# Memory attention, then a mixture of experts: z and M loaded once per batch, the first k and beta on the scalar queue, PSUM banks taken in turn by name, and a new step order

## The chip, the core and the metric

The kernel runs on one core of a Trainium2 chip. Five engines with a queue each work beside one another: TensorE (PE, matrix products and transposes), VectorE (DVE), ScalarE (ACT), GpSimd (POOL) and SyncE (SP, which here only issues transfers). An engine takes its instructions in order and waits at the head of its queue until the semaphores that an instruction names are there. The metric is the time of one execution on the device in microseconds (us), from three runs.

## The reference

Softmax attention and a linear memory are mixed by a gate per head; a router normalised eight times spreads the result over eight experts.

```python
B, H, S, D = 4, 8, 576, 64
a = softmax(where(causal, -1e9, scale * q @ k.T))
local = a @ v
phi = lambda x: where(x > 0, x, exp(x) - 1) + 1
mem_out = (phi(q) @ M_prev) / (phi(q) . z_prev + 1e-6)
g = 1 / (1 + exp(-beta))                    # one number for each head
x = g * mem_out + (1 - g) * local           # (2304, 512)
P = exp(x @ w_gate - max); 8 times: rows, then columns of P normalised, P *= N / E
out = sum over e of P[:, e] * (relu(x @ w1[e]) @ w2[e])
```

## The kernel before, in words

**Attention.** The 32 (batch, head) problems are taken as 16 pairs, pair p holding heads 2hp and 2hp+1 of batch b (`b, hp = divmod(p, 4)`), one head in each half of the 128 partitions. A pair is some 70 small steps that `steps(p)` names: `lq`, `lk`, `lv`, `lz`, `lm` load q, k, v, z_prev and M_prev by transfers of SP; `tq`, `tk`, `t5` transpose q and k on PE; `hq`, `hk`, `h5` (ACT) and `l_q`, `l_k`, `l5` (DVE) split them into a high and a low part; `s2`, `s3`, `s1`, `s4` are the scores of the row tiles (three products each); `m` (DVE) masks and takes the maxima; `x` (ACT) is the exponential with its sums; `rd`, `rv`, `rm` (DVE) make the reciprocals `rr` of the sums; `tr` transposes `rr`; `t30`, `t31`, `t20`, `t21`, `t1`, `t0`, `t4` transpose the exponentials, and `c..`, `d..`, `e0`, `e1` copy them from PSUM to `eA`, `eB`, `e1`, `e3`, `e4t`, on ACT or DVE as the table `TAKE` says; `fe`, `fm`, `fa`, `fz`, `ns`, `nr` are phi(q) and its norm against z; `gn`, `gp`, `tn`, `tp`, `cn`, `cp` scale and transpose phi; `v0` and `v1` are the products with v and M_prev in the PSUM bank `x`, `cx`, `km`, `kh`, `kl` take them out into the tensors `xh` and `xl`.

**Order.** Nothing is scheduled by the compiler here. Each step of pair p has the place p + WHEN[name] (+ LATER); all steps of all pairs are sorted by it, and each engine's queue is what remains of that list. A step that belongs to pair p can thus stand after steps of pair p + 1. From place 5.33 on, pieces of the first expert (`first1`, `first2`: products of PE in the bank `f`, 12 or 6 of 512 columns) are set between the steps, two for each pair, and the router's logits; pairs 1 to 4 have no such piece and are called plain below.

**Buffers.** The program uses eight PSUM banks: `x`, `f` and six that `ps_s()` hands out (tag `s`, bufs=6) to the transposes and the scores. A step that is given a bank waits until the readers of what stood there are through. `eA`, `eB`, `e1`, `e3`, `e4t` and `tmp` exist once; q, k and v are loaded into two buffers each. `z` has two buffers and three transfers a pair (a broadcast over 128 partitions and two halves of 64), `M_prev` three buffers and two transfers a pair. The start sends beta (in `setup_gates`) and then pair 0's q, z and k through SP.

**After attention** the expert loop (`experts`) has six products of 512 columns or twelve of 384 back to back on PE, in 71 items.

Of the kernel before, what the change touches and what calls it, by code (L numbers as in the profile page):

```python
# [17 lines left out]
def kernel(  # L18
# [70 lines left out]
    gt = ca.tile([128, 2, H], F32, name="gt")  # L89

    def ps_s():
        return ps.tile([128, 512], F32, tag="s", name="s", bufs=6)

    ps_t = ps_s

    def f32(ap):
# [3 lines left out]
    def w_task(j):  # L100
        dst = slots[0]
        if j < 2:
            hi, lo = (dst[a][:, 2 * j:2 * j + 2].rearrange("p k f -> p (k f)")
                      for a in ("w1h", "w1l"))
        else:
            hi, lo = dst["w2h"][:, j - 2], dst["w2l"][:, j - 2]
        raw = []

        def load():
            raw.append(wst_p.tile([128, 512], F32, tag="wst", name="wst"))  # L110
# [32 lines left out]

    def setup_gates():
        nc.sync.dma_start(
            out=gt[:, 0, :], in_=beta.rearrange("(o h) -> o h", o=1).to_broadcast([128, H])
        )
        nc.scalar.activation(out=gt[:, 0, :], in_=gt[:, 0, :], func=AF.Exp, scale=-1.0)
        nc.vector.tensor_scalar_add(gt[:, 0, :], gt[:, 0, :], 1.0)
# [12 lines left out]
    def setup_router():  # L162
        nc.vector.memset(f32(wgp), 0.0)
        wgr = wst_p.tile([128, 512], F32, tag="wst", name="wst")
# [10 lines left out]
    WHEN = {  # L175
# [15 lines left out]
    }  # L191
    LATER = {
    }
    TAKE = {
        "c30": "A", "c31": "D", "e0": "D", "e1": "A", "c20": "A", "c21": "D", "c1": "A",
        "d1": "D", "c0": "A", "d0": "D", "c4": "A", "d4": "D",
    }


    def attention():  # L200
        with ExitStack() as actx:
# [7 lines left out]
            )  # L209
            zb2 = [ap1.tile([128, 2, 128], F32, name=f"zb{j}") for j in range(2)]  # L210
            mraw = [ap1.tile([128, 128], F32, name=f"mraw{j}") for j in range(3)]
            eA = ap1.tile([128, 2, GA], F32, name="eA")
# [7 lines left out]
            for t_ in (*qraw, *kraw, *vraw):  # L220
                nc.vector.memset(t_[:, 4, :], 0.0)
            for t_ in (*mraw, *zb2, qn4, e4t):
                nc.vector.memset(t_, 0.0)
# [16 lines left out]

            def load_kv(p, src, dst):
                b, hp = divmod(p, HP)
                for h in range(2):
                    nc.sync.dma_start(
                        out=dst[:, 0:4, half[h]],
                        in_=src[b, 2 * hp + h, 0:512, :].rearrange("(t p) d -> p t d", p=128),
                    )
                nc.sync.dma_start(
                    out=dst[0:64, 4, :].rearrange("p (h d) -> p h d", h=2),
                    in_=src[b, 2 * hp:2 * hp + 2, 512:576, :].rearrange("h p d -> p h d"),  # L250
                )

            def load_z(p):
                b, hp = divmod(p, HP)
                nc.sync.dma_start(
                    out=zb2[p % 2][:, 0, :],
                    in_=z_prev[b, 2 * hp:2 * hp + 2, :].rearrange("(o h) d -> o (h d)", o=1)
                    .to_broadcast([128, 128]),
                )
                for h in range(2):  # L260
                    nc.sync.dma_start(
                        out=zb2[p % 2][half[h], 1, half[h]],
                        in_=z_prev[b, 2 * hp + h:2 * hp + h + 1, :].to_broadcast([64, 64]),
                    )

            def load_m(p):
                b, hp = divmod(p, HP)
                for h in range(2):
                    nc.sync.dma_start(out=mraw[p % 3][half[h], half[h]], in_=m_prev[b, 2 * hp + h])

            copy_ = {"A": nc.scalar.copy, "D": nc.vector.tensor_copy}

            def steps(p):
# [14 lines left out]

                step("lq")(lambda: load_q(p))
                step("lk")(lambda: load_kv(p, k, kraw[p % 2]))  # L290
                step("lv")(lambda: load_kv(p, v, vraw[p % 2]))
                step("lz")(lambda: load_z(p))
                step("lm")(lambda: load_m(p))

# [36 lines left out]

                zb = zb2[p % 2]

                @step("fe")
# [17 lines left out]
                def _():  # L352
                    nc.gpsimd.tensor_tensor(
                        out=s["tmp"][:, 0:4], in0=s["phi"][:, 0:4],
                        in1=zb[:, 0:1].to_broadcast([128, 4, 128]), op=ALU.mult,
                    )
                    nc.gpsimd.tensor_tensor(
                        out=s["tmp"][:, 4], in0=s["phi"][:, 4], in1=zb[:, 1], op=ALU.mult
                    )

                @step("ns")
                def _():
# [4 lines left out]
                    )  # L367
                    nc.vector.reduce_sum(rm[:, 8:9], tmp[:, 4], axis=AX.X)

# [15 lines left out]
                def scores(name, tiles):  # L385
# [19 lines left out]
                    for i in tiles:  # L405
# [4 lines left out]
                        def _(i=i, w=w, c0=c0):  # L410
                            sp = s.pop(("s", i))
                            s["e", i] = et = ap1.tile(
                                [128, 2, 512], F32, tag="e", name="e", bufs=4
                            )
# [153 lines left out]

                @step("tr")
                def _():  # L570
                    s["tr"] = t_ = ps_t()
                    nc.tensor.transpose(t_[0:9, 0:128], s["rr"][:, 2], ident)

                @step("tn")
                def _():
                    nc.tensor.transpose(s["tr"][:, 128:256], qn4, ident)

# [41 lines left out]
                for grp in range(2):  # L619
# [5 lines left out]
                    def _(grp=grp, w=w):  # L625
# [14 lines left out]
                        for h in range(2):  # L640
                            nc.tensor.matmul(  # L641
                                out=x[half[h], 0:256], lhsT=mraw[p % 3][:, half[h]],
                                rhs=qp[:, 256 * grp:256 * grp + 256], start=False,
                                stop=(grp == 0),
                            )
                        if grp:
                            for h in range(2):
                                nc.tensor.matmul(
                                    out=x[half[h], 256:320], lhsT=mraw[p % 3][:, half[h]],
                                    rhs=qp[:, 512 + 64 * h:576 + 64 * h], start=False, stop=True,  # L650
# [27 lines left out]
            for c, parts in enumerate(early_parts()):  # L678
# [7 lines left out]
            seq.append((WHEN["sg"], setup_gates))  # L686
            seq.append((1.0, setup_router))
# [143 lines left out]
    def first2(c, j, ps_new):  # L831
# [6 lines left out]
        def take():  # L838
            yst = wst_p.tile([128, DM], F32, tag="wst", name="wst")
            nc.vector.tensor_copy(out=yst, in_=bank[0])  # L840
            bank.append(yst)
# [362 lines left out]
```

## Time and profile before

| | |
|---|---|
| median of three runs | 1743.95 us (1743.18 to 1744.05) |
| the profiled execution's own time | 1743.34 us |
| its span, first to last instruction | 1741.5 us |
| PE busy | 1714.7 us, 98% of the span |
| attention, to 260.4 us | PE idle for 21 us |
| expert loop, from 260.4 us | PE idle for 5.8 us |

An engine's busy time is the union of its instructions' spans. The chain of waits goes back from the last instruction to whatever released it, so a line's share in it is the time that this line held up the end. The idle time before an instruction is put down to the semaphore that came last.

### The profile page before, as it was taken

To read this page: it belongs to the slowest core of one execution; us is meant where nothing else is said; L and a number is where in the kernel's file an instruction comes from. 1 tells how busy PE (TensorE), PEld (TensorE's weight loads), DVE (VectorE), ACT (ScalarE), POOL (GpSimd) and SP (SyncE) were. 2 spreads that over 40 slices of the span, in tenths; PEclk is the share of its full clock that TensorE was granted. 3 is DMA by queue.
4 is the path that set the end of the run, shared out by engine and by line. 5 is a ranking of instruction groups with operands and counts; after the bars stand their busy time and mean duration, and the time that the engine had idled before them with its cause. 6 is when DMAs were issued, how large, how long until landed. Compare 5 with 4: busy or idle time off the path is not lost.

```text
span 1741.5 us, 26964 instructions
## 1 busy us (share of the span) xinstructions
PE 1714.7 (98%) x9381; PEld 1524.1 (88%) x9381; DVE 1266.8 (73%) x2359; ACT 693.7 (40%) x1568; POOL 1154.5 (66%) x1107
## 2 busy tenths in 40 slices
PE   6899999999999999999999999999999999999999
PEld 5687778899999999989999999998899999999998
DVE  7877865877777777777777777777777777777776
ACT  5767752343333333234333333333343333333332
POOL 3855654477667777567767677665766777767673
PEclk9999999999999999999999999999999999999999
DMA  4433425122122221223222221222242222222211
GB/s 110 108 99 95 117 61 167 52 73 61 61 73 73 73 62 62 77 86 120 61 67 73 73 69 60 66 73 73 65 132 71 73 73 65 63 67 73 73 61 49
DMA packets 154888, 135.55 MB, mean 78 GB/s; under 512 B 71424, under 2 KB 121728, under 8 KB 154752
## 3 DMA queue, kind: packets, MB, share of 16 engines
q1 hardware_dynamic: 154320, 133.05, 25.9%
q8 instruction: 74, 1.21, 0.3%
q10 hardware_dynamic: 432, 0.79, 0.1%
q14 instruction: 62, 0.51, 0.1%
HBM read 124.28 MB, written 9.51 MB: 77 GB/s over the span
## 4 chain that ended last, share of the span: by engine, by line
PE 93%; DVE 1%; ACT 1%; DMA 0%; issue 0%; POOL 0%; SPq 0%; ACTq 0%; POOLq 0%; DVEq 0%
PE s L826 44%; PE s L1012 29%; PE f L1012 10%; PE x L636 2%; PE s L397 1%; PE s L478 1%; PE f L805 1%; PE f L826 1%; PE s L444 1%; PE x L641 1%; PE s L703 0%; PE s L805 0%; PE s L300 0%; PE s L529 0%; DMA raw<-in_moe_w_dram 0%
## 5 line engine op out<-in xcount | busy, mean ns | idle before, releaser
L963 POOL TENSOR_TENSOR w1l<-raw,w1h 128x512 fp32r<-128x512 f32 x263 | 366.4, 1407 | 395.3 <-ACT w1h L962 391.2
L1083 DVE SCALAR_TENSOR_TENSOR acc<-s,P,acc 128x512 f32<-128x512 f32 x540 | 395.2, 744 | 145.2 <-PE s L826 145.2
L826 PE MATMUL s<-w2h,hhl 128*128 128x512 f32 x1116 | 436.1, 391 | 0.0
L826 PE MATMUL s<-w2l,hhh 128*128 128x512 f32 x1116 | 435.8, 391 | 0.0
L826 PE MATMUL s<-w2h,hhh 128*128 128x512 f32 x1116 | 435.0, 390 | 0.0
L1043 DVE TENSOR_TENSOR temps<-s,temps 128x384 f32<-128x384 f32 x447 | 242.6, 555 | 172.9 <-ACT w1h L962 85.1
L997 DVE SCALAR_TENSOR_TENSOR hhl<-temps,hhh 128x384 fp32r<-128x384 f32 x340 | 306.5, 901 | 0.0
L986 POOL TENSOR_TENSOR w2l<-raw,w2h 128x512 fp32r<-128x512 f32 x186 | 293.3, 1598 | 9.8 <-ACT w2h L985 9.8
L996 ACT ACTIVATE hhh<-temps 128x384 fp32r<-128x384 f32 x340 | 178.6, 525 | 296.9 <-DVE temps L1043 289.4
L826 PEld LDWEIGHTS s<-w2h,hhl 128*128 128x128 f32 x1116 | 209.4, 188 | 43.9
L826 PEld LDWEIGHTS s<-w2h,hhh 128*128 128x128 f32 x1116 | 209.6, 188 | 42.7 <-DVE acc L1083 1.5
L826 PEld LDWEIGHTS s<-w2l,hhh 128*128 128x128 f32 x1116 | 209.4, 188 | 41.6
L1046 ACT COPY temps<-s 128x384 f32<-128x384 f32 x64 | 30.7, 480 | 415.7 <-PE s L1012 408.9
L1012 PE MATMUL s<-th,w1h 128*128 128x384 f32 x510 | 170.3, 334 | 0.0
L1012 PE MATMUL s<-tl,w1h 128*128 128x384 f32 x510 | 170.3, 334 | 0.0
L1012 PE MATMUL s<-th,w1l 128*128 128x384 f32 x510 | 170.3, 334 | 0.0
L1012 PE MATMUL s<-xh,w1l 128*128 128x384 f32 x480 | 161.3, 336 | 0.4 <-POOL w1l L958 0.4
L1012 PE MATMUL s<-xh,w1h 128*128 128x384 f32 x480 | 161.3, 336 | 0.0
L1012 PE MATMUL s<-xl,w1h 128*128 128x384 f32 x480 | 160.8, 335 | 0.0
L962 ACT CAST w1h<-raw 128x512 fp32r<-128x512 f32 x263 | 154.0, 615 | 2.9 <-issue 2.9
L1043 DVE TENSOR_TENSOR temps<-f,temps 128x384 f32<-128x384 f32 x148 | 80.3, 555 | 57.5 <-PE f L1012 27.9
L985 ACT CAST w2h<-raw 128x512 fp32r<-128x512 f32 x186 | 111.9, 607 | 0.0
(218 smaller groups left out, 2873.1 us busy)
## 6 DMA issues: line engine op xcount, KB each, us to landing
raw<-in_moe_w_dram SPq DMA_DIRECT2D x372, 256.0 KB
rsb<-rd SPq DMA_DIRECT2D x32, 144.0 KB
ydr<-wst SPq DMA_DIRECT2D x18, 256.0 KB
acc<-ydr SPq DMA_DIRECT2D x18, 256.0 KB
qraw<-in_q_dram SPq DMA_DIRECT2D x32, 128.0 KB
kraw<-in_k_dram SPq DMA_DIRECT2D x32, 128.0 KB
vraw<-in_v_dram SPq DMA_DIRECT2D x32, 128.0 KB
out_dram<-acc SPq DMA_DIRECT2D x15, 256.0 KB
```

Of the source, the lines that this page charges most:

```text
L636: nc.tensor.matmul(out=x[half[h], a0:a1], lhsT=vs[:, kt, h], rhs=ee(h), start=(kt == 0), stop=False,)
L826: nc.tensor.matmul(out=pt, lhsT=h_[:, f, cols], rhs=w[:, f], start=(n == 0), stop=(n == 5))
L962: nc.scalar.copy(out=wh[:, i:i + 2], in_=src)
L963: tt(out=wl[:, i:i + 2], in0=src, in1=f32(wh[:, i:i + 2]), op=ALU.subtract)
L985: nc.scalar.copy(out=wh[:, j], in_=raws[j])
L986: nc.gpsimd.tensor_tensor(out=wl[:, j], in0=raws[j], in1=f32(wh[:, j]), op=ALU.subtract)
L996: nc.scalar.activation(out=hh[:, f, c], in_=src, func=AF.Relu)
L997: late.append(lambda: nc.vector.scalar_tensor_tensor(out=hl[:, f, c], in0=src, scalar=0.0, in1=f32(hh[:, f, c]), op0=ALU.max, op1=ALU.subt ...
L1012: nc.tensor.matmul(out=pt[:, 0:HT], lhsT=w[:, wi, k], rhs=x[:, k], start=(n == 0), stop=(n == total - 1),)
L1043: nc.vector.tensor_tensor(out=o, in0=x, in1=y, op=ALU.add)
L1046: nc.scalar.copy(out=X, in_=prod(q, [(0, b11)]))
L1083: nc.vector.scalar_tensor_tensor(out=acc[:, j], in0=pt, scalar=P[:, t_, e:e + 1], in1=acc[:, j], op0=ALU.mult, op1=ALU.add,)
```

## The change

- `load_z` and `load_m` run once per batch (`hp == 0`): one broadcast transfer of 512 numbers to 128 partitions (`zb`), and two transfers that fill `mb` for four pairs, in place of twelve and eight. `fz` is one GpSimd instruction over 640 columns and not two of 512 and 128. `ns` reduces the two half tiles of row tile 4 apart.
- `setup_gates` loses its transfer: `load_gates` (place -2.255) issues beta on ACT's queue. Pair 0's k is issued on ACT's queue too.
- `ps_s()` and the staging tiles take their buffers in turn by name (`s0` to `s5`, `wst0`, `wst1`), and the exponentials' tiles have a name for each row tile.
- The bank of `tr` and `tn` is taken by whichever comes first.
- `WHEN` has new numbers throughout, `LATER` gets 24 shifts for pairs 0, 1 and 15, and `TAKE` moves `c21`, `d1`, `d0` and `d4` from DVE to ACT and swaps `e0` (now ACT) and `e1` (now DVE).

```diff
 def ps_s():
-    return ps.tile([128, 512], F32, tag="s", name="s", bufs=6)
+    turn[0] += 1
+    return ps.tile([128, 512], F32, tag=f"s{turn[0] % 6}", name="s", bufs=1)
...
-def setup_gates():
-    nc.sync.dma_start(
+def load_gates():
+    nc.scalar.dma_start(
...
-    step("lk")(lambda: load_kv(p, k, kraw[p % 2]))
+    step("lk")(lambda: load_kv(p, k, kraw[p % 2], nc.sync if p else nc.scalar))
...
-    step("lz")(lambda: load_z(p))
-    step("lm")(lambda: load_m(p))
+    if hp == 0:
+        step("lz")(lambda: load_z(p // HP))
+        step("lm")(lambda: load_m(p // HP))
...
     nc.gpsimd.tensor_tensor(
-        out=s["tmp"][:, 0:4], in0=s["phi"][:, 0:4],
-        in1=zb[:, 0:1].to_broadcast([128, 4, 128]), op=ALU.mult,
-    )
-    nc.gpsimd.tensor_tensor(
-        out=s["tmp"][:, 4], in0=s["phi"][:, 4], in1=zb[:, 1], op=ALU.mult
+        out=s["tmp"], in0=s["phi"],
+        in1=zb[:, hp:hp + 1].to_broadcast([128, 5, 128]), op=ALU.mult,
     )
...
-    nc.vector.reduce_sum(rm[:, 8:9], tmp[:, 4], axis=AX.X)
+    for h in range(2):
+        nc.vector.reduce_sum(
+            rm[half[h], 8:9], tmp[half[h], 4, half[h]], axis=AX.X
+        )
...
-    "c30": "A", "c31": "D", "e0": "D", "e1": "A", "c20": "A", "c21": "D", "c1": "A",
-    "d1": "D", "c0": "A", "d0": "D", "c4": "A", "d4": "D",
+    "c30": "A", "c31": "D", "e0": "A", "e1": "D", "c20": "A", "c21": "A", "c1": "A",
+    "d1": "A", "c0": "A", "d0": "A", "c4": "A", "d4": "A",
```

What the tables make of the queues, at three places. `L469` before and `L480` after is the helper that does the copies of `TAKE`.

ACT at the start of the program, before: the table load, a first exponential, the gate's exponential (`gt`), then pair 0's `fe`, `hq`, `h5`, `hk`.

```order
L142 ACT_TABLE_LOAD
L142 ACTIVATE mx<-ones 128x1
L148 ACTIVATE gt<-gt 128x8
L337 ACTIVATE tmp<-qraw_119 128x640
L304 CAST qh<-s 128x512
L323 CAST kh<-s 128x64
```

The same place after, with beta's transfer ahead of the table load and k's three between the two exponentials.

```order
L154 DMA gt<-in_beta_dram 128x8
L151 ACT_TABLE_LOAD
L151 ACTIVATE mx<-ones 128x1
L261 DMA kraw_121<-in_k_dram 128x4x64 x2
L265 DMA kraw_121<-in_k_dram 64x2x64
L159 ACTIVATE gt<-gt 128x8
L348 ACTIVATE tmp<-qraw_119 128x640
L317 CAST qh<-s 128x512
L317 CAST kh<-s 128x512
```

k's transfers leave SP and stand on ACT, ahead of the gate's exponential, for which DVE's first steps wait.

DVE in a plain pair before, around the reciprocals: `nr` (the last instruction of it), `rd`, the next pair's `l_q`, `rv`, `rm`, `cr`, and after that parts of `l5`, `d4` and `l_k`.

```order
L375 TENSOR_TENSOR rm<-rm,gcol 128x9
L543 TENSOR_SCALAR rr<-sum 128x9
L287 TENSOR_TENSOR ql<-s,qh 128x512
L550 RECIPROCAL rr<-rr 128x9
L548 TENSOR_TENSOR rr<-rm,rr 128x9
L580 COPY rt<-s 9x128
L287 TENSOR_TENSOR kl<-s,kh 128x64
```

The same place after, from `fa` of the next pair on.

```order
L357 SCALAR_TENSOR_TENSOR phi<-qraw_119,tmp 128x640
L554 TENSOR_SCALAR rr<-sum 128x9
L561 RECIPROCAL rr<-rr 128x9
L559 TENSOR_TENSOR rr<-rm,rr 128x9
L299 TENSOR_TENSOR ql<-s,qh 128x512
L299 TENSOR_TENSOR kl<-s,kh 128x512
```

The next pair's `l_q`, which waits for ACT's `hq`, stood between `rd` and `rv`; now `rd`, `rv` and `rm` stand together ahead of it.

PE in a plain pair before, from `tr` to the next pair's scores: `tr`, `t4`, `t30`, `t1`, `tn`, `t0` (two rows), `tp`, `t31`, then `s2` of the next pair.

```order
L572 MATMUL s<-ident,rr 9x128
L529 MATMUL s<-ident,e_135 128x128 x4
L478 MATMUL s<-ident,e 128x128 x4
L497 MATMUL s<-ident,e 128x128 x4
L576 MATMUL s<-ident,qn_136 128x128
L511 MATMUL s<-ident,e 128x128 x2
L514 MATMUL s<-ident,e_135 64x128
L611 MATMUL s<-ident,phi 128x128 x4
L478 MATMUL s<-ident,e 128x128 x4
L397 MATMUL s<-kh,qh 128x384 x2
```

The same place after: `tr`, then `t30`, `t31` and `t20` in one row, `tn`, `t4`, `t1`, `t0`, `s2`.

```order
L586 MATMUL s<-ident,rr 9x128
L489 MATMUL s<-ident,e 128x128 x11
L588 MATMUL s<-ident,qn_133 128x128
L540 MATMUL s<-ident,e_132 128x128 x4
L508 MATMUL s<-ident,e 128x128 x4
L522 MATMUL s<-ident,e 128x128 x2
L525 MATMUL s<-ident,e_132 64x128
L408 MATMUL s<-kh,qh 128x384 x2
```

`tp` has left this place (it stands behind the next pair's `s1` now), `t20` has come here from before `tr`, and `t31` has moved from the end to the front.

## Rows read from the trace of the kernel before

**Rows 1.** The page: busy times by engine, and the chain that ended last

```profile
PE 1714.7 (98%) x9381; PEld 1524.1 (88%) x9381; DVE 1266.8 (73%) x2359; ACT 693.7 (40%) x1568; POOL 1154.5 (66%) x1107
...
PE 93%; DVE 1%; ACT 1%; DMA 0%; issue 0%; POOL 0%; SPq 0%; ACTq 0%; POOLq 0%; DVEq 0%
```

**Rows 2.** Stretches: length; busy of PE, PEld, DVE, ACT, POOL; clock; DMA; GB/s

```profile
0.00:26.80 26.80, 14.84 (x81) 12.14 (x82) 18.20 (x72) 13.58 (x37) 8.76 (x19) 0.94 0.43 95
26.80:82.95 56.15, 50.15 (x446) 38.53 (x445) 47.05 (x170) 41.38 (x127) 39.59 (x51) 1.00 0.46 114
82.95:260.44 177.49, 174.50 (x1429) 139.24 (x1428) 133.75 (x481) 118.92 (x361) 100.86 (x139) 1.00 0.36 94
260.44:1741.50 1481.06, 1475.26 (x7429) 1334.19 (x7429) 1067.81 (x1638) 519.82 (x1045) 1005.31 (x899) 1.00 0.24 74
...
23.64:27.05 3.41, 3.41 (x18) 2.78 (x18) 2.56 (x8) 2.10 (x6) 2.08 (x2) 0.50 0.30 56
```

**Rows 3.** What PE waited for: total us, times, longest

```profile
PE s L572 <- DVE rr L548: 5.2, 5, 2.2
...
PE s L317 <- DMA kraw<-in_k_dram: 3.5, 1, 3.5
PE s L611 <- DVE e L469: 2.2, 4, 0.6
...
PE s L300 <- DVE mn L454: 1.1, 1, 1.1
...
PE s L723 <- ACT ls L711: 0.7, 1, 0.7
```

**Rows 4.** Timeline, SP at the start: start, us taken, engine, line, names

```profile
0.74 0.39 SPq L145 DMA_DIRECT2D gt<-in_beta_dram  x1
...
5.20 1.14 SPq L244 DMA_DIRECT2D kraw<-in_k_dram  x2
6.38 0.66 SPq L248 DMA_DIRECT2D kraw<-in_k_dram  x1
```

**Rows 5.** Timeline of ACT, DVE and PE at the start, to the second pair's scores

```profile
2.02 0.20 ACT L142 ACTIVATE mx<-ones 128x1 f32<-128x1 f32 x1
...
3.58 0.17 DVE L149 TENSOR_SCALAR gt<-gt 128x8 f32<-128x8 f32 x1 [0.49 <-ACT gt L148]
...
6.98 0.69 DVE L287 TENSOR_TENSOR ql<-s,qh 128x512 fp32r<-128x512 f32 x1
...
8.98 0.45 PE L317 MATMUL s<-ident,kraw 128*128 128x128 f32 x1 [3.53 <-DMA kraw<-in_k_dram]
...
11.89 0.69 PE L397 MATMUL s<-kl,qh 64*128 64x384 f32 x2
...
26.80 0.55 PE L397 MATMUL s<-kh,qh 64*128 64x384 f32 x2
```

**Rows 6.** Timeline of DVE and PE in a plain pair

```profile
50.40 0.69 DVE L287 TENSOR_TENSOR ql<-s,qh 128x512 fp32r<-128x512 f32 x1 [0.18 <-ACT qh L304]
...
51.00 0.20 DVE L550 RECIPROCAL rr<-rr 128x9 f32<-128x9 f32 x1
...
51.26 0.28 PE L572 MATMUL s<-ident,rr 128*9 128x128 f32 x1 [0.79 <-DVE rr L548]
```

**Rows 7.** The copies in 37.18:79.27: xcount, busy us, mean ns, idle before

```profile
L469 ACT COPY eB<-s 128x384 f32<-128x384 f32 x9 | 4.0, 482 | 2.6 <-PE s L478 2.5
...
L469 ACT COPY eA<-s 128x256 f32<-128x256 f32 x6 | 2.2, 373 | 4.1 <-DVE e L469 4.1
...
L469 ACT COPY e<-s 128x128 f32<-128x128 f32 x3 | 0.8, 283 | 0.0
...
L469 DVE COPY eB<-s 128x384 f32<-128x384 f32 x6 | 3.3, 556 | 0.5 <-ACT e L469 0.5
...
L469 DVE COPY e<-s 128x128 f32<-128x128 f32 x6 | 1.7, 287 | 3.7 <-ACT eB L469 3.7
...
L469 DVE COPY e<-s 128x256 f32<-128x256 f32 x3 | 1.2, 415 | 0.0
```

More of the change, by code (lines that the diff above doesn't have):

```diff
@@ L89, with wst @@
     gt = ca.tile([128, 2, H], F32, name="gt")
+    turn = [0]
     def ps_s():
-        return ps.tile([128, 512], F32, tag="s", name="s", bufs=6)
+        turn[0] += 1
+        return ps.tile([128, 512], F32, tag=f"s{turn[0] % 6}", name="s", bufs=1)
     ps_t = ps_s
+    wturn = [0]
+    def wst(w=512):
+        wturn[0] += 1
+        return wst_p.tile([128, w], F32, tag=f"wst{wturn[0] % 2}", name="wst", bufs=1)
     def f32(ap):
@@ L109, in load @@
         def load():
-            raw.append(wst_p.tile([128, 512], F32, tag="wst", name="wst"))
+            raw.append(wst())
             if j < 2:
@@ L142, in setup, with setup_gates @@
         nc.scalar.activation(out=mx[:, 0:1], in_=ones[:, 0:1], func=AF.Exp)
-    def setup_gates():
-        nc.sync.dma_start(
+    def load_gates():
+        nc.scalar.dma_start(
             out=gt[:, 0, :], in_=beta.rearrange("(o h) -> o h", o=1).to_broadcast([128, H])
         )
+    def setup_gates():
         nc.scalar.activation(out=gt[:, 0, :], in_=gt[:, 0, :], func=AF.Exp, scale=-1.0)
@@ L163, in setup_router @@
         nc.vector.memset(f32(wgp), 0.0)
-        wgr = wst_p.tile([128, 512], F32, tag="wst", name="wst")
+        wgr = wst()
         wgv = wgr[:, 0:KD * E].rearrange("p (k e) -> p k e", e=E)
@@ L209, in attention @@
             )
-            zb2 = [ap1.tile([128, 2, 128], F32, name=f"zb{j}") for j in range(2)]
-            mraw = [ap1.tile([128, 128], F32, name=f"mraw{j}") for j in range(3)]
+            zb = ap1.tile([128, HP, 128], F32, name="zb")
+            mb = ap1.tile([128, HP, 128], F32, name="mb")
             eA = ap1.tile([128, 2, GA], F32, name="eA")
@@ L221, in attention @@
                 nc.vector.memset(t_[:, 4, :], 0.0)
-            for t_ in (*mraw, *zb2, qn4, e4t):
+            for t_ in (mb, qn4, e4t):
                 nc.vector.memset(t_, 0.0)
@@ L239, in load_q, with load_kv @@
                     )
-            def load_kv(p, src, dst):
+            def load_kv(p, src, dst, eng=nc.sync):
                 b, hp = divmod(p, HP)
                 for h in range(2):
-                    nc.sync.dma_start(
+                    eng.dma_start(
                         out=dst[:, 0:4, half[h]],
@@ L247, in load_kv @@
                     )
-                nc.sync.dma_start(
+                eng.dma_start(
                     out=dst[0:64, 4, :].rearrange("p (h d) -> p h d", h=2),
@@ L251, in load_kv, with load_z, load_m @@
                 )
-            def load_z(p):
-                b, hp = divmod(p, HP)
+            def load_z(b):
                 nc.sync.dma_start(
-                    out=zb2[p % 2][:, 0, :],
-                    in_=z_prev[b, 2 * hp:2 * hp + 2, :].rearrange("(o h) d -> o (h d)", o=1)
-                    .to_broadcast([128, 128]),
+                    out=zb.rearrange("p x d -> p (x d)"),
+                    in_=z_prev[b].rearrange("(o h) d -> o (h d)", o=1).to_broadcast([128, H * D]),
                 )
+            def load_m(b):
                 for h in range(2):
                     nc.sync.dma_start(
-                        out=zb2[p % 2][half[h], 1, half[h]],
-                        in_=z_prev[b, 2 * hp + h:2 * hp + h + 1, :].to_broadcast([64, 64]),
-                    )
[L266 to L269, printed above, removed]
+                        out=mb[half[h], :, half[h]],
+                        in_=m_prev[b, h:H:2].rearrange("x d e -> d x e"),
+                    )
             copy_ = {"A": nc.scalar.copy, "D": nc.vector.tensor_copy}
@@ L330, in _ @@
                     sub(kl[:, 576:704], t_[:, 128:256], s["kh"][:, 576:704])
-                zb = zb2[p % 2]
                 @step("fe")
@@ L412, in _ @@
                             s["e", i] = et = ap1.tile(
-                                [128, 2, 512], F32, tag="e", name="e", bufs=4
+                                [128, 2, 512], F32, tag=f"et{i}", name="e", bufs=1
                             )
@@ L567, in _, with tr_ @@
                     )
[L569 to L576, printed above, removed]
+                def tr_():
+                    if "tr" not in s:
+                        s["tr"] = ps_t()
+                    return s["tr"]
+                step("tr")(
+                    lambda: nc.tensor.transpose(tr_()[0:9, 0:128], s["rr"][:, 2], ident)
+                )
+                step("tn")(lambda: nc.tensor.transpose(tr_()[:, 128:256], qn4, ident))
                 @step("cr")
@@ L641, in _ @@
                             nc.tensor.matmul(
-                                out=x[half[h], 0:256], lhsT=mraw[p % 3][:, half[h]],
+                                out=x[half[h], 0:256], lhsT=mb[:, hp, half[h]],
                                 rhs=qp[:, 256 * grp:256 * grp + 256], start=False,
@@ L648, in _ @@
                                 nc.tensor.matmul(
-                                    out=x[half[h], 256:320], lhsT=mraw[p % 3][:, half[h]],
+                                    out=x[half[h], 256:320], lhsT=mb[:, hp, half[h]],
                                     rhs=qp[:, 512 + 64 * h:576 + 64 * h], start=False, stop=True,
@@ L685, in attention @@
                     seq += [(t0 + WHEN.get(a, 0.0), f) for a, f in zip(kinds, fs)]
-            seq.append((WHEN["sg"], setup_gates))
+            seq += [(WHEN["sl"], load_gates), (WHEN["sg"], setup_gates)]
             seq.append((1.0, setup_router))
@@ L838, in take @@
         def take():
-            yst = wst_p.tile([128, DM], F32, tag="wst", name="wst")
+            yst = wst(DM)
             nc.vector.tensor_copy(out=yst, in_=bank[0])
```

36 rows, old and new, of tables (LATER, WHEN) are left out of this document.

## The prediction

> **What bounds the kernel now.** I read the page's busy times and its chain first [rows 1]: PE is busy for 98% of the span and holds 93% of the chain, so only time in which PE idles, or runs at the lower clock, can be won; the number of products doesn't change. Then the stretches [rows 2], to see where the 27 us of PE's idle time lie. The expert loop has 5.8 us of it in 1481 (1481.06 - 1475.26) and no line of it is changed. Attention has 21: 12.0 up to the second pair's scores (26.80 - 14.84), 6.0 in the four plain pairs (56.15 - 50.15), and 3.0 in the pairs that carry expert pieces (177.49 - 174.50). What may change is therefore in the first 260 us. Then what PE waited for there [rows 3]: the reciprocals of the sums before `tr` (L572, five times), the first k (3.5 us), the copies before `tp` (L611), and a bank in pair 0. Last the timeline at the two places where these waits lie [rows 4 to 6].
>
> **First k (term 1).** SP issues pair 0's k at 5.20, behind eight other transfers (beta, four of q, three of z), and its last part, issued at 6.38, lets PE go on at 8.98, 2.60 later [rows 4, 5]. After, ACT issues it. ACT is through with the table load and its first exponential at 2.22 (2.02 + 0.20); beta's issue ahead costs 0.39 [rows 4], so k is issued from 2.61, two in 1.14 and one in 0.66, the last from 3.75: it lands at about 6.35, some 2.6 earlier. But ACT comes to the gate's exponential only after the third issue, at 4.41, and DVE's first steps wait for that: they begin at about 4.65 (4.41, the exponential's 0.20 and a little) instead of 3.58. From 3.58 to the end of `l_q` at 7.67 (6.98 + 0.69) they took 4.09, so `l_q` ends at 8.74, and `l_k`, another 0.69 by the row of `l_q` (the same operation and size), at 9.4. PE's second score product, which waits for `l_k`, started at 11.89 [rows 5]. So DVE, not k, is the late one then, and the gain is **2.5 us**. It is 3.0 if the half microsecond in which DVE waited inside those 4.09 closes up, and 0 if k's and q's transfers, now under way together, hold each other up by those 2.6.
>
> The Trainium skill speaks against this edit: by "DMA: Bandwidth & Descriptors", section "Issuing engines are not separate DMA queues", transfers from several engines interleave on the same DMA engines, and a second issuer saves only issue time. By it q and k would slow each other, the term would go toward 0 and the sum to -10.2, which is rival D. The trace bears that out little: what stands ahead of k there is 4.46 us of SP's issuing (5.20 - 0.74) [rows 4].
>
> **Rest of pair 0 (term 2).** Up to the second scores at 26.80 PE waits 1.1 for a bank and 2.2 for the reciprocals, and from 23.64 to 27.05 it runs at half clock (0.50, that is 1.2 of 2.4 GHz), after a stretch with gaps and mostly transposes [rows 2, 3]. At full clock these 3.41 us of dense work would take 1.7. The new order lets more of `tq`, `tk`, `t5` and `t30` stand ahead of `tr`, and puts the reciprocals ahead of `l_q`; the chain scores, maxima, exponentials, reciprocals stays as long as ACT and DVE make it. I take back **2.0 us**, half way between nothing and all of it: 0 to 4.5.
>
> **Plain pairs (term 3).** The four take 14.06, 14.08, 14.45 and 13.56 (56.15 in sum), with 12.54 of PE each [rows 2]. The first of them shows two idle places that the order removes. `rv` (0.20 at 51.00) stands behind the next pair's `l_q` (0.69 at 50.40), which itself waits for ACT; PE waits 0.79 for it at 51.26 [rows 6]. After, `rd`, `rv`, `rm` stand ahead of `l_q`. `tp` waits 0.55 in each pair for a bank that a DVE copy holds (L611) [rows 3]; it goes behind the next `s1`, where six banks have been turned over. `v0` and `v1` move behind the next pair's `tp` and `t5`, where their copies are long through.
>
> What replaces them is ACT. `TAKE` gives it `c21` (128x384, 0.482), `d1` (128x256, 0.373), `d4` and `d0` (128x128 or less, 0.283 each), 1.42 in sum; `e0` for `e1` is even [rows 7]. It has 41.38 / 4 = 10.35 now, so 11.8 then. DVE has 47.05 / 4 = 11.76 and loses 0.556 + 0.415 + 2 x 0.287 = 1.55, and gets perhaps 0.2 for `ns` in three reductions: 10.4. So neither is above PE's 12.54, and the engines' loads come to PE's own time as the bound. I take **12.5 a pair: 56.15 - 50.0 = 6.2 us**. The ends: 11.8, ACT's load, since PE's busy spans overlap the filling of the array and hide some slack, gives 9.3; 13.6, the shortest plain pair of the trace, gives 1.8.
>
> **Pairs with expert pieces (term 4).** PE idles 3.0 in 177.49 [rows 2], among it 0.7 for the logits' copy (L723) [rows 3], ahead of which the last pair's `v1` now stands, and shares of the waits named above. I take **2.0**; from a gain of 4 (all of it and some hidden slack) to the loss of rival C.
>
> **At nothing.** SP issues 5 transfers fewer in three pairs of four; by the row of k's third issue, 0.66 each, that is 3.3 us a pair of a queue that no PE wait names after the start. `fz` saves one GpSimd instruction; GpSimd has 9.9 of 14 us. If these covers were gone they would be gains, so nothing is lost. Named banks: the turn of six over 20 grants a pair is that of the bufs=6 rotation; its price is in the waits above. The expert loop, with its staging tiles by name: 0, within 1 either way.
>
> **Sum.** -2.5 - 2.0 - 6.2 - 2.0 = -12.7. The profiled execution's own time is 1743.34, of which 1.8 lies around the span and stays: 1730.6. The median of the runs is 0.6 above that execution, so **1731 us**.
>
> **The rivals.** *A, ACT becomes the bound:* its queue is in order, and after `v1` it has `c21`, `e0`, `cx1`, `c30`, `c20`, `c4`, `d4`, `c1`, `c0`, `d1`, `d0` in a row, whose banks the next scores need. By rows 7 (`cx1` taken as the 0.482 of the nearest size) these eleven make 4.4 us in a row, a third of the period, and the third score tile waits for the last of them. If that wait keeps plain pairs at 13.6, and the later pairs gain nothing, it is -2.5 - 2.0 - 1.8 = -6.3: 1737.6. For it: ACT at 11.8 of 12.5 has no slack for a wait. Against: now both ACT and DVE wait for each other at these copies, and the new list has nearly all on one engine.
>
> *B, the clock falls in the denser transposes:* the block `tr` to `t0` is transposes alone, as was the work before 23.64. If PE fell to 0.50 once in every pair up to the fifth, pair 0 would win nothing for it (+1.7) and the four plain pairs would lose 1.7 each (+6.8): -4.2, 1739.8. Against: the plain pairs now stand at 1.00 with the same transposes [rows 2]. The Trainium skill, "TensorE: Matmul & The Clock Gate", section "Part 4: PE-mode transpose", says that a transpose doesn't count as busy for the clock in the way a product does; by that rule this rival would come true wherever transposes fill a stretch, and the trace bears it out only in pair 0.
>
> *C, slower:* with expert pieces the second piece of a pair stands between `tn` and `t4`, and ACT's relu of it stands ahead of `c4`, `d4`, `c1`, `c0`, `d1`, `d0` and of the next pair's first exponentials. If that tail of ACT reaches past PE's next scores by 1.5 us in each of 11 pairs, it costs 16.5; the plain pairs, with the same queue, then gain nothing either, and -4.5 of terms 1 and 2 is left: +12, 1755. It decides from an overhang of 0.7 us a pair on: 11 x 0.7 covers the 4.5 and 3.5 more. ACT's 118.92 in 177.49 speaks against: two thirds busy.
>
> *D, k gains nothing on ACT's queue* (it lands at 8.98 still): -10.2, 1733.
>
> **Chances.** Forecast, 1724 to 1737: 0.56. A: 0.17. B: 0.06. C: 0.08. D: 0.08. More than 20 us won, if hidden slack in PE's busy spans is larger than I take it: 0.05. The range 1721 to 1740 leaves out C, the last, half of B and a little of A, some 0.18. About 0.2%, 3.5 us, is what a measurement of this kernel can tell from no change; so faster (under 1740.5) has the forecast, D, the last and most of A and B: 0.87; the same 0.05; slower 0.08.
>
> **What would show it.** Right: in the profile after, PE's first score product that waits for `l_k` starts at 9 to 9.6, not 11.9; the second pair's scores at 21.5 to 23; the next four pairs stand 12 to 13 us apart; `tr` (L586) and `tp` (L623) are gone from the list of PE's waits; the expert loop's length is 1481 as before. Wrong: plain pairs of 13.5 or more with PE waiting for ACT's copies at the third score tile (A); a granted clock of 0.50 after 27 us (B); ACT waiting for `f` and PE for ACT in the pairs with pieces (C); k landing at 9 (D). The forecast fails if the four plain pairs keep 14 us, since half of it is there.

## The result, and the profile after

The changed kernel takes 1727.7 us (median of 4 runs, 1727.6 to 1728.3) against 1743.6 before: ratio 0.991, 95% interval 0.989 to 0.993. The forecast was 1731, with a range from 1721 to 1740. The profiled span is 1725.8 against 1741.5, 15.7 less.

The page after: busy time by engine, and the chain that ended last [rows 1].

```profile
PE 1707.8 (99%) x9381; PEld 1519.2 (88%) x9381; DVE 1250.3 (72%) x2307; ACT 707.1 (41%) x1632; POOL 1148.6 (67%) x1091
...
PE 97%; DVE 1%; DMA 1%; ACT 1%; POOL 0%; issue 0%; SPq 0%; POOLq 0%; ACTq 0%; DVEq 0%
```

PE has the same 9381 products, and 97% of the chain instead of 93%. The stretches after, cut where a pair's scores begin (pair 0; pair 1; 2; 3; 4; the filled pairs 5 to 14; the rest), with the columns of [rows 2]:

```profile
0.00:21.27 21.27, 12.29 (x77) 10.78 (x77) 16.70 (x66) 13.03 (x38) 8.96 (x18) 1.00 0.63 143
21.27:35.89 14.62, 12.30 (x112) 9.46 (x111) 13.86 (x43) 11.15 (x37) 9.13 (x11) 1.00 0.46 119
35.89:47.99 12.10, 11.92 (x112) 9.43 (x112) 11.40 (x40) 11.22 (x38) 10.61 (x14) 1.00 0.52 122
47.99:59.70 11.71, 11.71 (x113) 9.46 (x112) 10.85 (x40) 10.93 (x36) 9.45 (x13) 1.00 0.55 126
59.70:71.53 11.83, 11.83 (x114) 9.51 (x113) 10.36 (x40) 11.37 (x39) 8.57 (x12) 1.00 0.50 113
71.53:224.20 152.67, 152.67 (x1267) 121.44 (x1266) 113.75 (x413) 117.40 (x370) 88.29 (x115) 1.00 0.37 94
224.20:1725.80 1501.60, 1495.06 (x7595) 1349.10 (x7594) 1073.36 (x1671) 531.95 (x1084) 1013.61 (x914) 1.00 0.24 74
```

The second pair's scores begin at 21.27 instead of 26.80 (-5.5), the four plain pairs take 50.26 instead of 56.15 (-5.9), and all behind them 1654.3 (152.67 + 1501.60) instead of 1658.6 [rows 2] (-4.3). From the fourth pair to 224.20 PE has no idle time left. What PE still waits for in attention, with the columns of [rows 3]:

```profile
PE s L313 <- DMA qraw<-in_q_dram: 4.7, 1, 4.7
PE s L586 <- DVE rr L559: 3.2, 3, 2.6
PE s L623 <- DVE mn L428: 1.7, 1, 1.7
PE s L330 <- DMA kraw<-in_k_dram: 1.6, 1, 1.6
```

The wait of `tr` for the reciprocals (now L586) is left in three places instead of five, 2.6 of it in pair 0, and the four of `tp` for a copy (L611) are gone. New is the third row: `tp` waits once, in the second pair, for a maximum of DVE. The timeline there, DVE, GpSimd and PE, shows why:

```profile
22.24 0.48 DVE L174 MEMSET wgp<- 128x512 f32 x1 [0.17 <-issue]
22.76 1.51 DVE L178 CAST wgp<-wst 128x32 fp32r<-128x32 f32 x1
...
22.69 1.54 POOL L391 TENSOR_TENSOR vs<-vraw,ogb 128x640 f32<-128x640 f32 x1
...
25.12 0.63 PE L623 MATMUL s<-ident,phi 128*128 128x128 f32 x4 [1.72 <-DVE mn L428]
```

The router's set-up stands at place 1.0, now ahead of the pair's first maxima, and its cast of 32 elements, which took 0.18 in the kernel before, takes 1.51 and ends with GpSimd's product (24.27 and 24.23). Without it the plain pairs would have gained more.

At the start (ACT's issue, DVE, PE):

```profile
1.22 1.28 ACT L151 ACT_TABLE_LOAD   x1 [1.22 <-PEq L1200]
1.28 1.09 ACTq L261 DMA_DIRECT2D kraw<-in_k_dram  x2
...
4.00 0.69 ACTq L265 DMA_DIRECT2D kraw<-in_k_dram  x1
...
7.82 0.68 DVE L299 TENSOR_TENSOR ql<-s,qh 128x512 fp32r<-128x512 f32 x1
8.42 0.68 DVE L299 TENSOR_TENSOR kl<-s,kh 128x512 fp32r<-128x512 f32 x1
...
8.29 0.45 PE L330 MATMUL s<-ident,kraw 128*128 128x128 f32 x1 [1.64 <-DMA kraw<-in_k_dram]
...
8.88 0.69 PE L408 MATMUL s<-kh,qh 64*128 64x384 f32 x2
9.37 0.52 PE L408 MATMUL s<-kl,qh 64*128 64x384 f32 x2
```

The first product that reads `kl` starts at 9.37, not 11.89 [rows 5].

### The profile page after: what moved, and what is told of

Same layout as the page of the kernel before. It is cut to its first block, busy times and chain, and to the rows that moved or that the text cites. A ratio compares the mean times of both kernels' runs of the same rounds, so it can differ in the third digit from the quotient of the medians.

```text
span 1725.8 us, 26878 instructions
## 1 busy us (share of the span) xinstructions
PE 1707.8 (99%) x9381; PEld 1519.2 (88%) x9381; DVE 1250.3 (72%) x2307; ACT 707.1 (41%) x1632; POOL 1148.6 (67%) x1091
## 3 DMA queue, kind: packets, MB, share of 16 engines
q10 hardware_dynamic: 1776, 1.09, 0.2%
## 4 chain that ended last, share of the span: by engine, by line
PE 97%; DVE 1%; DMA 1%; ACT 1%; POOL 0%; issue 0%; SPq 0%; POOLq 0%; ACTq 0%; DVEq 0%
PE s L838 44%; PE s L1024 30%; PE f L1024 10%; PE x L648 2%; PE s L408 2%; PE s L489 1%; PE f L838 1%; PE f L817 1%; PE s L313 1%; PE s L455 1%; PE x L653 1%; PE s L623 1%; PE s L715 0%; PE s L540 0%; PE s L508 0%; PE s L817 0%
```

## The experiments

All times in one table: the median, and from each trace the start of the first product that reads `kl`, the start of the second pair's scores, the length of the second pair (pair 1), of the next three, and of the ten filled pairs behind them.

| kernel | us | kl | 2nd scores | pair 1 | pairs 2-4 | filled |
|---|---|---|---|---|---|---|
| before | 1743.6 | 11.89 | 26.80 | 14.06 | 42.09 | 156.59 |
| after | 1727.7 | 9.37 | 21.27 | 14.62 | 35.64 | 152.67 |
| order_only | 1732.6 | 11.34 | 25.43 | 15.22 | 35.60 | 152.68 |
| loads_only | 1746.9 | 11.47 | 27.01 | 14.59 | 42.70 | 158.77 |
| loads_old_banks | 1745.5 | 10.94 | 25.10 | 14.61 | 42.71 | 158.55 |
| k_on_sp | 1728.4 | 8.88 | 23.34 | 13.28 | 35.54 | 152.66 |
| zm_per_pair | 1731.7 | 9.22 | 23.14 | 16.38 | 35.76 | 152.65 |
| take_only | 1760.8 | 11.88 | 26.19 | 16.82 | 47.71 | 164.36 |
| old_take | 1767.9 | 9.55 | 23.40 | 13.51 | 42.73 | 180.53 |
| lq_back | 1729.5 | 9.46 | 23.29 | 13.74 | 36.20 | 152.69 |
| tp_back | 1780.0 | 9.25 | 23.26 | 17.03 | 49.36 | 183.21 |
| held_ops | 1727.0 | 9.19 | 21.72 | 13.28 | 35.64 | 152.67 |
| best | 1728.5 | 9.11 | 22.57 | 14.41 | 35.55 | 152.71 |
| best3 | 1726.3 | 9.49 | 21.97 | 12.80 | 35.62 | 152.67 |

**The order, or the loads?** order_only is the kernel before with the new `WHEN`, `LATER` and `TAKE`. Its tables differ from those of the changed kernel in the places of z, M and the first k, which stay on SP:

```diff
-        ... "lz": -0.494, "lm": 0.887, ...
+        ... "lz": -1.25, "lm": 0.217, ...
...
-        ... (0, "lk"): -0.662, (0, "lz"): -0.094, ...
+        ... (0, "lk"): 0.361, ...
```

> The kernel before with the new tables (order of the steps and ACT/DVE shares) alone: z and M are loaded per pair as before, k and beta stay on SP, the banks are the old rotation of six. Theory (the order carries it): everything but the first k is there, so the second score product starts at 11.9 as before, the second pair's scores 3 us earlier than before (23.8), the four plain pairs take 50.3 +-0.5, the filled stretch 152.7 +-0.5, and the time is 1730.5 (1729.5 to 1731.5), 2.5 behind the whole change. Rival (SP's relief carries it): SP's five transfers more in three pairs of four hold the reciprocals' way through memory or the next loads, the plain pairs keep 13 us or more and the time is 1736 or above.

Measured 1732.6, ratio 0.994 (0.992 to 0.995). From the third pair on it is the changed kernel, within 0.1: the order with its shares carries these 10.4 (6.5 and 3.9). But it is 4.7 behind at the end of pair 4, not 2.5. Only 2.0 of that is the first k; the rest lies in pairs 0 and 1: PE waits 3.7 for the reciprocals instead of 2.6, and behind that wait the granted clock falls to 0.50 for 3.4, which costs 1.7. The second scores come at 25.43, not the 23.8 expected. loads_only is the reverse, the changed kernel with the old tables, and loads_old_banks that with the rotation of six:

```diff
-        return ps.tile([128, 512], F32, tag=f"s{turn[0] % 6}", name="s", bufs=1)
+        return ps.tile([128, 512], F32, tag="s", name="s", bufs=6)
```

> The changed kernel with the old tables, so only the loads and named banks are new (z and M once per batch, k and beta of pair 0 on ACT's queue). Theory (the order carries the pairs): second score product at 9.4, second pair's scores 2.5 earlier than before (24.3), plain pairs 56.1 as before, filled stretch 156.6 as before; the time is 1741 (1740 to 1742). Rival (SP's relief): plain pairs of 13 and the time 1736 or below.

> The kernel with the old tables and the new loads once more, now with the old rotation of six PSUM buffers instead of the six names. With the names, tp of a plain pair waited 1.15 for the bank that l_k reads, where in the kernel before it waited 0.55 for a bank that a copy of ACT's or DVE's reads. Theory (the turn by name is fixed, the rotation takes what comes free, and with the old order the fixed turn hits a late bank): tp's wait goes back to 0.55, the plain pairs to 56.1 and the filled stretch to 156.6, the time falls from 1746.9 to 1743 (1742 to 1744.5). Rival (the names cost nothing and the once-a-batch loads do): it stays at 1746 to 1747.5.

loads_only is slower than before, not faster: 1746.9 against the 1741 expected, ratio 1.002 (1.001 to 1.003). Its product with `kl` starts at 11.47 although k is issued early, since the old order has `tk` behind `t5` and ACT's and DVE's work on `kh` after that. With the rotation it is 1745.5, 1.3 less, between what theory and rival expected. But that is not shown to be a price of the names. `tp`, which waited 1.15 in a plain pair, waits 0.55 again, as the theory had it, and yet the pairs stay as long (42.70 and 42.71, 158.77 and 158.55). The difference lies ahead of the second scores, 1.9: 0.5 of it is there at the product with `kl` (11.47 and 10.94), and the rest comes of the clock, which falls behind the reciprocals in loads_only and stays at 1.00 in loads_old_banks. The same transposes there, loads_only first:

```profile
22.99 1.06 PE L484 MATMUL s<-ident,e 128*128 128x128 f32 x4
...
22.04 0.60 PE L484 MATMUL s<-ident,e 128*128 128x128 f32 x4
```

The other 1.8 stay with the once-a-batch loads and the old order; `ns`, three reductions instead of two on a loaded DVE, is a candidate that was not tried by itself, nor were the staging and exponential tiles, which keep their names here. So the two halves of the change give -11.1 and +3.2 alone, and -15.9 together.

**The first k.** In k_on_sp it is back on SP, right behind q:

```diff
-                step("lk")(lambda: load_kv(p, k, kraw[p % 2], nc.sync if p else nc.scalar))
+                step("lk")(lambda: load_kv(p, k, kraw[p % 2]))
-        (0, "lk"): -0.662,
+        (0, "lk"): 0.361,
```

> The changed kernel with pair 0's k back on SP's queue, right behind q's four transfers and ahead of z; beta stays on ACT. Theory (what counted was the place of k in the line, not the second queue): SP issues k from 3.0, its last part at about 4.2 and it lands at 7.2 to 8.3; ACT is free for the gate's exponential at about 3 instead of 4.74, q lands earlier for having the wires to itself (5.0 instead of 5.78); the second score product starts within 0.7 of 9.37, and the time is 1727.7 +-0.7. Rival (the queue itself counted): k lands at 9 or later and the time is 1730 or above.

Measured 1728.4. The theory holds: 8.88, half a microsecond earlier than with two queues. It is the place in the line that counts. What it wins there is lost again by the second pair's scores (23.34): `tr` starts at 19.80 instead of 18.98, and behind it the clock falls to 0.50 from 20.5 to 24. DVE, GpSimd and PE there:

```profile
18.37 1.13 DVE L554 TENSOR_SCALAR rr<-sum 128x9 f32<-128x9 f32 x1
...
17.93 1.53 POOL L364 TENSOR_TENSOR tmp<-phi,zb 128x640 f32<-128x640 f32 x1 [2.88 <-DVE phi L357]
...
19.80 0.28 PE L586 MATMUL s<-ident,rr 128*9 128x128 f32 x1 [3.25 <-DVE rr L559]
```

`rd`, nine elements wide, is held until GpSimd's product ends.

**SP's load.** zm_per_pair loads z and M in every pair again, with the two GpSimd products and the two reductions that belong to it.

> The changed kernel with z and M loaded per pair again (five transfers in each pair, two GpSimd instructions for phi times z, the old two reductions), k and beta still on ACT. Theory (SP has slack once the first pair is through): within 1 of the changed kernel's 1727.7; plain pairs 50.3 +-0.5. Rival: SP's 3.3 us more a pair show up in the reciprocals' way through memory (rt, rd, rsb) or in late loads, 0.5 a pair, and the time is 1735.

Measured 1731.7, 4.0 slower, and both theory (within 1) and rival (1735) missed. The loss is in the first two pairs alone (1.9 to the second scores, 1.8 in the second pair); from the third on there is none, and there the theory was right. At the start SP's queue has no lead yet. v is issued at 11.62 instead of 8.74, and GpSimd's product `vs` starts at 15.43 instead of 12.41, beside the last operation of pair 0's `nr`, which takes 1.32 instead of 0.17; `tr` starts 0.5 later, and the other 1.4 come behind it, where the clock falls (20 to 23.5). In the second pair the router's weights land late (DVE, GpSimd):

```profile
15.67 1.32 DVE L391 TENSOR_TENSOR rm<-rm,gcol 128x9 f32<-128x9 f32 x1
...
15.43 1.53 POOL L396 TENSOR_TENSOR vs<-vraw,ogb 128x640 f32<-128x640 f32 x1 [5.20 <-DVE rm L389]
...
26.00 0.30 DVE L178 CAST wgp<-wst 128x32 fp32r<-128x32 f32 x1 [2.83 <-DMA wst<-in_moe_w_gate_dram]
26.34 1.47 DVE L179 TENSOR_TENSOR wgp<-wst,wgp 128x32 fp32r<-128x32 f32 x1
```

**The shares.** take_only is the kernel before with the new `TAKE`; old_take the changed kernel with the old one.

> The kernel before with the new shares of ACT and DVE in the copies (c21, d1, d4 and d0 to ACT, e0 and e1 exchanged) and nothing else. Theory (a share pays only with the order made for it): the copies given to ACT stand in its queue between the old exponentials, and the time is within 5 of 1743.7, on either side. Rival (the shares carry the gain, as giving them back cost 40 in the changed kernel): plain pairs of 13 or less and the time 1736 or below.

> The changed kernel with the old shares of ACT and DVE in the copies (c21, d1, d4 and d0 back on DVE, e0 and e1 exchanged); order and loads are the new ones. DVE has 10.4 to 10.9 in the plain pairs of the changed kernel and gets 1.4 back. Theory (the order carries the gain, the shares only keep both engines below PE's 11.7): DVE's load of about 12.2 becomes the bound of the plain pairs, +0.5 in each, the filled pairs (13.9 each) have room; the time is 1730 (1728.5 to 1732). Rival (the shares carry it, since the two engines wait for each other at these copies): plain pairs of 13 or more, the filled stretch back above 155, the time 1735 or above. Second rival (the shares don't matter): within 0.7 of 1727.7.

Both are slower by far: 1760.8 (ratio 1.010, 1.008 to 1.011) and 1767.9, 40 above the changed kernel. Both theories missed the size, since they reckoned with loads and not with queues; in old_take it is the rival (1735 or above) that came. In the old order the new copies stand on ACT between the exponentials (`c21` waits there for PE, and five exponentials behind it), and `tr` waits for the sums (take_only); in the new order the old shares put `d0` and `d1` on DVE beside the next pair's first maxima, and the scores wait for the banks that they read (old_take):

```profile
49.93 0.48 ACT L469 COPY eB<-s 128x384 f32<-128x384 f32 x1 [2.29 <-PE x L636]
...
PE s L572 <- DVE rr L548: 20.3, 10, 3.4
```

```profile
PE s L408 <- DVE e4t L480: 11.9, 14, 0.9
PE s L408 <- DVE e L480: 7.2, 12, 0.8
```

In pairs 2 to 4 DVE is busy for 32.6 in the changed kernel and 35.6 in old_take, 1.0 more a pair, which leaves it below the 13.5 to 15.4 that a pair then takes; the position is what costs. Falls of the clock come on top: in attention it goes to 0.50 four times in take_only and six times in old_take, 1.7 lost each time.

**Two places of the order.** lq_back puts `l_q` between `rd` and `rv` again, tp_back puts `tp` ahead of the next scores:

```diff
-        ... "l_q": -0.432, ...
+        ... "l_q": -0.54, ...
...
-        ... (1, "l_q"): -0.147,
```

```diff
-        ... "tp": 1.174, ...
+        ... "tp": 0.99, ...
...
-        ... (15, "tp"): -0.255, ...
+        ... (15, "tp"): -0.071, ...
```

> The changed kernel with l_q back between rd and rv, its place in the kernel before, in all pairs. There PE waited 0.8 for the reciprocals in each plain pair. In the changed kernel rv ends at 56.17 in the fourth pair and tr starts at 56.98, since v1 now stands ahead of tr on PE, so 0.8 is free. Theory (v1 ahead of tr hides l_q's 0.69 anyway): plain pairs within 0.2 of 11.75, the time 1728 to 1729 (pair 0, which has no v1, loses 0.6). Rival (moving l_q is what took the wait away): +0.7 in each plain pair and part of it in the others, the time 1731 to 1738.

> The changed kernel with tp back ahead of the next pair's scores in all pairs. In the kernel before it waited 0.55 there for a bank that a DVE copy held. In the changed kernel phi's last product on GpSimd, which tp reads, ends at 59.63 in the fourth pair, 0.07 ahead of the next scores at 59.70. Theory (tp goes ahead of work that doesn't need it): it waits for GpSimd or for a bank, 0.3 to 0.8 in each plain pair and some in the others, the time 1730 to 1735. Rival (the copies on ACT have cleared the banks, and the move is worth nothing): within 0.7 of 1727.7.

lq_back: 1729.5, half a microsecond above the theory's range. Pairs 2 to 4 lose 0.56 in sum and the filled ones nothing, so there `v1` ahead of `tr` hides most of `l_q`'s 0.69 a pair, as the theory had it. In pair 0, which has no `v1`, 2.0 are lost: `tr` starts 0.5 later, and the clock falls from 19 to 22.5; the second pair gives 0.9 back. tp_back: 1780.0 (its runs spread from 1769.5 to 1784.6), ratio 1.020, far beyond both expectations. `cp` was left where it stands, behind the next pair's first exponentials, and one of `s1`'s banks is, by the turn of six, that of `tp`. PE and ACT in a plain pair:

```profile
60.54 0.49 PE L408 MATMUL s<-kh,qh 64*128 64x256 f32 x1 [1.72 <-ACT qp L627]
...
59.92 0.56 ACT L627 COPY qp<-s 128x512 f32<-128x512 f32 x1
```

After such waits the clock falls too (0.80 on average from 40 to 80). Whether `tp` with `cp` beside it would do better ahead of the scores wasn't tried.

**The held operations.** held_ops moves the router's set-up and one GpSimd step:

```diff
-            seq.append((1.0, setup_router))
+            seq.append((6.365, setup_router))
-        (1, "fz"): -0.212,
+        (1, "fz"): 0.102,
```

> The changed kernel with two steps at other places: the router's set-up (three small DVE operations) goes from the second pair to behind the seventh, and the second pair's GpSimd product of phi and z from ahead of rd of pair 0 to behind gp of pair 0. In the profile after, the set-up's cast of 32 elements took 1.51 until GpSimd's product vs ended, and rd of pair 0 took 0.57 until GpSimd's product with z ended; before, the same two took 0.18 and 0.17. Theory (DVE's small SBUF operations are held while GpSimd's tensor operation runs): rd takes 0.17 and PE's wait in pair 0 falls by 0.4; the wait of 1.7 for the maxima in the second pair is gone; the time is 1725.7 (1725.2 to 1726.6). Rival (the lengths are the trace's, and the maxima wait for something else): the waits stay and the time is within 0.5 of 1727.7.

Measured 1727.0, between theory and rival. Both waits went as expected: `rd` takes 0.16 where no GpSimd operation runs, and the second pair 13.28 instead of 14.62. In the same trace `rd` of the next pair is held, beside GpSimd (DVE, then GpSimd):

```profile
17.91 0.16 DVE L554 TENSOR_SCALAR rr<-sum 128x9 f32<-128x9 f32 x1
...
30.23 1.40 DVE L554 TENSOR_SCALAR rr<-sum 128x9 f32<-128x9 f32 x1 [0.26 <-ACT e L474]
...
30.05 1.55 POOL L364 TENSOR_TENSOR tmp<-phi,zb 128x640 f32<-128x640 f32 x1 [2.98 <-DVE phi L357]
```

The gain is only 0.7 because the clock falls in pair 0 (stretches of PE's clock, third column from the end):

```profile
18.00:20.00 2.00, 1.63 (x13) 1.63 (x14) 1.86 (x10) 1.38 (x4) 1.43 (x3) 0.88 0.35 78
20.00:22.00 2.00, 2.00 (x11) 1.62 (x11) 0.79 (x3) 1.19 (x4) 2.00 (x3) 0.50 0.01 2
22.00:24.00 2.00, 2.00 (x22) 1.89 (x22) 1.67 (x6) 1.63 (x5) 1.92 (x3) 0.77 0.70 202
```

**Two tries at a better kernel.** best has held_ops' two moves (in its expectation "the run before last"), a new start, and the second pair's `hq` behind pair 0's last exponential; best3 moves the same steps, keeps the changed kernel's loads and puts `fz` between `gn` and `gp`:

```diff
-        (1, "fz"): -0.212, (1, "gn"): 0.017, (1, "hq"): -0.089, (1, "l_q"): -0.147,
+        (1, "fz"): 0.052, (1, "gn"): 0.017, (1, "l_q"): -0.09,
```

> The changed kernel with the two moves of the run before last and a new start: SP issues the four large transfers of q and k of pair 0 first, then the three small ones; z of the first batch goes on ACT's queue behind beta; in pair 0 fe, fm and fa stand behind hk and l_k; the second pair's hq stands behind the last exponential of pair 0, and its l_q behind rd and rv. Theory: k's large parts land at about 5.4 and PE's second score product starts at 7.9 instead of 9.37 (-1.5), the exponentials of pair 0 end 1.0 to 1.3 earlier relative to their start, PE's wait for the reciprocals falls from 2.6 to 1 or 1.5, and with the 2.1 of the held operations the time is 1723 (1721.5 to 1725). Rival (DVE's work up to rd bounds pair 0, whatever lands first): the second scores start at 20 or later and the time is 1725 to 1726.5.

> The changed kernel, loads and all, with three steps moved: the router's set-up behind the seventh pair, the second pair's GpSimd product of phi and z between gn and gp of pair 0, and the second pair's hq behind the last exponential of pair 0 (with its l_q behind rd and rv). Theory: the exponentials of pair 0 lose the 0.8 in which ACT waits for hq's transposes and hq's own 0.5, so PE's wait for the reciprocals falls to 1.5 or less and PE keeps its full clock; second scores at 20.1 to 20.5 instead of 21.27, the second pair 13.3 instead of 14.6; the time is 1725.5 (1724.8 to 1726.3). Rival (the clock falls again in pair 0, as it did with the first two of these moves): second scores at 21.5 and the time 1727.

best, 1728.5, above theory and rival: q's large parts land at 5.75 instead of 4.71. k's follow them at 1.77 and z's 256 KB go out at 1.28, where the changed kernel has k at 1.28 and z at 3.00; which of the two holds q up wasn't tried. And with `fe`, `fm` and `fa` behind `l_k` GpSimd's `fz` and then `ns` end so late that the first maximum starts at 13.14 instead of 10.80. best3, 1726.3: PE's wait for the reciprocals is 1.7 (1.5 was hoped for) and the second pair 12.80 (13.3), but the clock falls from 18 to 21.5, as the rival had it, and the second scores come at 21.97. It is the fastest kernel here, by 1.4 or 0.08%, which the comparison can't tell from nothing.

## Why the prediction held, and where not

The forecast was 12.7 less, 15.9 came, and the terms were right in sign. Several were right or near for other reasons than those given.

**First k: 2.5 forecast, 2.52 measured, by luck.** The step "So DVE, not k, is the late one then" failed. DVE's `l_k` ends at 9.10 (forecast 9.4), and PE isn't there yet: `t5` stands ahead of the scores in its queue and waits until 8.29 for k's third part, and from 8.29 to 9.37 PE has no gap. ACT issued k's first two parts at 1.28, while its table load ran, and not behind it at 2.61; but the third went out at 4.00, and it took 4.29 to land instead of 2.60, with SP's loads of the second pair under way from 3.76 on. The caution that q and k slow each other came true in part: ACT's exponential of q (`fe`) waits for q until 5.78, and in k_on_sp starts at 4.69. Here the trace agrees with the Trainium skill ("DMA: Bandwidth & Descriptors", "Issuing engines are not separate DMA queues"), by which a second issuer saves issue time only: the second queue moved the issue from 3.00 to 1.28, yet the product with `kl` starts half a microsecond later than with SP alone. Rival D gave the queue no gain; that was wrong in time and right in kind.

**Rest of pair 0: 2.0 forecast, 3.0 measured** (5.53 - 2.52), inside its bounds (the three items named add up to 5.0, not 4.5). PE's wait for a bank fell from 1.1 to 0.2. And 1.7 is the half-clock stretch of [rows 2], which the changed kernel doesn't have. That wasn't earned by a shorter wait: PE waits 2.6 for the reciprocals, against 2.2 before, and keeps 1.00, while held_ops waits 2.3 and best3 1.7, and both fall to 0.50 (1.2 of 2.4 GHz); best, with 1.7 as well, keeps 1.00. Eleven of the fourteen kernels have a stretch of about 3.4 at half clock in or behind pair 0; the changed one, best and loads_old_banks don't, and what decides it stays open. "Half way between nothing and all of it" was a fair sum for a reason that the runs don't bear out.

**Plain pairs: 6.2 forecast, 5.89 measured, made up of two misses.** (The rows cited for the idle places, around 50 to 51, are those of the second of the four, not the first.) The step by which "the engines' loads come to PE's own time as the bound", 12.54, failed: pairs 3 and 4 take 11.71 and 11.83 with PE busy throughout, so the busy spans of before held 0.8 a pair that the same products don't need. The prediction had this slack as the end of its range only (and 11.8 a pair gives 9.0 there, not 9.3). Rows of a plain pair suggest where it sits, as an estimate: the transpose at 67.14 in the kernel before has a span of 0.27, and the next starts at 67.25, so each time PE stops behind one, up to 0.16 of waiting counts as busy. The second pair, 14.62, lost 1.3 of the gain again to the router's set-up, which the prediction didn't see moved ahead of the maxima on DVE; held_ops gives it back. In pairs 3 and 4 ACT has 10.9 and 11.4 and DVE 10.9 and 10.4, near what was reckoned (11.8 and 10.4).

**Filled pairs and the rest: 2.0 forecast, 4.3 measured**, just beyond the low end of 4. The same mis-sized step: PE's 3.0 of idle time was counted, and at least 1.3 more came out of spans that counted as busy.

**At nothing:** right for SP from the third pair on, wrong in the first two, where zm_per_pair is 4.0 slower: no PE wait named SP, but what SP brings late moves DVE and GpSimd into each other's way. Some 1.4 of the 4.0 is the clock's fall in pair 0, which so many kernels here have that it can't be laid on SP alone. The named banks cost nothing from the third pair on: order_only has the rotation and is within 0.1 there. That they cost anything with the old order isn't shown.

**The signs that were named.** `kl` at 9 to 9.6 came, and the expert loop's 1481. The second scores came a little earlier than 21.5. Missed were 12 to 13 for each of the four pairs (14.62, 12.10, 11.71, 11.83), and `tr` and `tp` gone from the list of waits: `tr` is still there with 3.2, and `tp` has a new wait of 1.7.

**The rivals.** A did not come, with ACT's list in the new order; with the same shares in the old order ACT held the plain pairs at 15.0 to 16.8 (take_only), though by way of the exponentials' sums and not at the third score tile. B: the clock stays at 1.00 in all plain pairs; in take_only, old_take and tp_back it falls in some of them. C: no wait for ACT in the filled pairs, though tp_back shows what an overhang of that kind costs. (The times given for C and D start from a base 0.6 below that of A and B, which changes no order among them.)

## What to carry to other kernels

An order, the engines' shares and the turn of the buffers are one solution: a single piece put back cost up to 52, and the shares or the loads alone are slower than the kernel before, so judge such pieces in the whole that they were made for. Take an engine's busy time as a floor only from a stretch in which it doesn't wait: here it hid 0.8 of 12.5. A gain at the start is worth what the next stage lets through: k half a microsecond earlier was gone by the second pair. And look for a stretch at half clock before comparing two variants: one such stretch, 1.7 here, is more than most of the differences between the better kernels.

## What was not expected of the hardware

Small DVE operations from SBUF to SBUF (`TENSOR_SCALAR`, `CAST`, `TENSOR_TENSOR` of two such inputs) stand still while GpSimd's tensor operation runs: 0.16 to 0.18 us became 0.57, 1.13, 1.32, 1.40 and 1.51, each ending within 0.05 of GpSimd's operation. Not all do: the changed kernel's two small reductions take 0.43 at 21.64, beside a GpSimd product, and 0.43 at 10.34 with none. The Trainium skill says so ("SBUF — State Buffer", "Who interferes with whom": operations of these kinds can contend with GpSimd, and then one of the two holds their shared ports for its whole instruction and the other waits, while a reduction doesn't contend), and these traces agree; the prediction hadn't drawn on it.

ACT's queue issues transfers while the engine loads its table (issue at 1.28, load from 1.22 to 2.50).

At the start the clock's column can't be read: it shows 1.00 there, while four transposes take 1.09 (4.71 in the changed kernel), and 0.60 from 15.10 on. What holds them at little over half speed the column doesn't say, so durations of equal products are the safer reading.
